# State products on four 64 by 64 quarters of TensorE, with x in two PSUM banks, in a retention, RWKV and Hyena kernel

## The chip, the cores and the metric

One core of one Trainium2 chip. The metric is device time in microseconds of one execution; before the change the median of three runs is 325.34 us (324.66 to 327.6). The profile is that of one further execution.

## What is computed

Three layers follow one another (batch 2, 768 tokens, model width 512 = 8 heads of 64):

```python
# 1: retention with decay, in blocks
intra = (qb @ kb.T * Dmask) @ vb
inter = (qb * lam_pow) @ kv_state
out[block] = intra + inter
kv_state = lam_block * kv_state + (kb * rev_pow).T @ vb
# 2: RWKV channel mix, x_prev is x one token earlier
xk = mu_k * x + (1 - mu_k) * x_prev;  xr = mu_r * x + (1 - mu_r) * x_prev
y = sigmoid(xr @ w_r) * (relu(xk @ w_k) ** 2 @ w_v)
# 3: Hyena: a causal convolution of 5 taps gates a projection
z = (sigmoid(conv(y)) * (y @ w_val)) @ w_out
```

The weights come as float64 and the kernel turns them into float32 itself; products of layers 2 and 3 are made of two float32r parts ("hi" and "lo", three products for one).

## The kernel before

**Tiling.** A chunk is 128 tokens (6 per batch row, 12 in all, numbered 0 to 11), a group is two chunks (256 tokens, 0 to 5). A head pair n (0 to 3) is 128 rows: heads 2n and 2n+1. Chunk 0 of each batch row has no state yet, so chunks 1 to 5 and 7 to 11 have products with a state.

**Attention of a chunk.** Step A (`attention_scores`) transposes k and q (on TensorE for groups 0 to 2, from blocks that a DMA brings, `kin` and `qin`, and a VectorE transpose for the others), decays k (`kt`), makes the scores `sc` and masks them into `p`. Step B (`attention_values`) makes the kv products `u` (L424), the new state (L440) and x (`attend`, L467): first the products of the state with the decayed q (`qd`), 64 rows by 64 columns each, then those of v with p, 128 rows by 64 columns. x of a chunk is one PSUM bank, `x[64*s:64*s+64, n, :]` for head s of pair n; there are two such tiles. `keep_x` (L495) copies it to SBUF.

**Layer 2** for a group: `mix` makes xr and xk from x (xrf, then the parts xrh on ScalarE, L519, and xrl on VectorE or GpSimd, L520), `ffn_r` the products psr, `ffn_k` psk and the squares kk, `ffn_v` psv. All products of layers 2 and 3 stand in `products` (L532), the last in `project` (L671).

**Weights.** w_r and w_k (12 pieces) and w_v (8 pieces) are loaded by `load_w`, one DMA for each piece of 256 rows by 256 columns (L250). A piece is then converted over three ticks: `start` on ScalarE (L167, L168), `bits` on VectorE (L172 to L174), `add` (L179), then whi on ScalarE (L184) and wlo (L187).

**What sets the order.** `LOADS` gives the first DMAs, all in one queue on SyncE. `STEPS` is written by hand: A, B, m, k, M (mixes), r, f, F, h, v (layer 2), t and w (a tick, a load), l (a late weight), G, S, V, P (layer 3); letters behind a number choose the engine. The framework schedules around this list and fixes each engine's order before the run. The loads of chunk c+2, and the 32 block DMAs of a group, are issued inside step A of chunk c (L756, `load_chunk`). Each DMA takes one of eight semaphores in turn, so it also waits until the transfer eight places earlier has landed.

Of the kernel before, what the change touches and what calls it, by code (L numbers as in the profile page):

```python
# [27 lines left out]

LOADS = """
    l k0 v0 q0 k1 q1 w1 M q2 v1 k2 w1 v2 q3 v3 k3 q4 w2 k4 v4 w1 v5 k5 q5 w5  # L30
""".split()
STEPS = """
    W2 c W10 A0vfd tgg A1a tgv B0 B1 A2f x0 B2 tgv A3d tvv tvv B3 m0.0dg tvv m0.1g A4au w m1.0g
    B4 A5af r0.1 r0.0 m1.1g B5 tvg w m2.0 m2.1d k0.0 t r1.0 r1.1 r2.0 t w t w k0.1 r2.1 tv f0.1s
    tvv tgv tvv k1.0 f0.3 k1.1d f0.0s k2.1 w k2.0 w tvv f0.2s tvv F1.1 F1.0sg w tvv w w F1.3s
    tvv F1.2 F2.0s w tvv F2.2s tgv h1.3 tgg F2.3 v0.0 C h1.0 tgv v0.1 F2.1sg A6ad B6v A7ad X
    h1.1 h1.2 v1.0 B7 h2.0 h2.1 x1 v1.1 h2.2 h2.3 v2.0 M3.0g M3.1 v2.1 A8vu A9u f3.3sg f3.1s
    f3.0s f3.2s B8 r3.0 v3.0 r3.1 B9v v3.1 M4.1g M4.0dg l1 r4.1 l1 r4.0 f4.0s A10f f4.1sg l1v
    f4.2s B10v A11au f4.3s G0.0 B11v v4.0 M5.0 M5.1d l1 l1v v4.1 f5.3s Z r5.1 l1 f5.0s r5.0 S0.0
    f5.1sg S1.0v l1 G0.1 f5.2s S0.1v v5.0 G1.0 V0.0 l1v V0.1 G2.1 S1.1v G1.1 P0.1 S3.0v P0.0  # L40
    V1.1 S2.1k V1.0 v5.1 S2.0v G3.1 P1.1 G2.0 S3.1v P1.0v V2.1 G3.0 V2.0 V3.1 G5.1 V3.0 P2.1v
    S5.0 G4.1 P2.0 P3.0 G5.0 S4.1vk S4.0k G4.0 V4.1 V4.0 S5.1vk P3.1 V5.0g V5.1 P4.0v P4.1 P5.0v
    P5.1.2v
# [4 lines left out]
def retention_rwkv_hyena_kernel(  # L48
# [102 lines left out]
    class Conversion:  # L151


        def __init__(self, raw, key=None, hi=None, lo=None, lo_engine=None, add_engine=None):
# [6 lines left out]
            self.add_engine = add_engine or GP  # L161
            self.age = 0
# [7 lines left out]
        def bits(self):  # L170
            x = self.x.bitcast(I32)
            V.tensor_scalar(self.x, self.x, LEAST, MOST, op0=ALU.max, op1=ALU.min)  # L172
# [60 lines left out]
    def load_w(n=1):  # L233
        for _ in range(n):
            if not to_load:
                return
# [8 lines left out]
            else:  # L245
# [4 lines left out]
            last_w[0] = nc.sync.dma_start(  # L250
                raws[key].rearrange("p (k f) -> p k f", k=2),
                sources[name][2 * row * P:(2 * row + 2) * P, 256 * col:256 * col + 256].rearrange(
                    "(k p) f -> p k f", p=P
                ),
            ).ins

    def tick_w(add=GP, lo=GP):
# [7 lines left out]
        else:  # L265
# [5 lines left out]
            lo, add_engine=add,  # L271
# [4 lines left out]
    def tick_late(n=1, lo=GP):  # L276

        for _ in range(n):
# [15 lines left out]
            tick(Conversion(raw, key, whi[key], wlo[key], lo))  # L294
# [4 lines left out]
    def load_qk(g):  # L299
# [3 lines left out]
        group[g] = {}  # L303
        for nm, src in (("k", k), ("q", q)):
            t = group[g][nm + "in"] = att_group_tile(f"{nm}in{g}")
            for n in range(NPAIR):
                for s in range(2):
                    for db in range(2):
                        p0 = 64 * s + 32 * db
                        nc.sync.dma_start(  # L310
                            t[p0:p0 + 32, n, :].rearrange("p (t e) -> p t e", e=32),
                            src[b, 2 * n + s, t0:t0 + G, 32 * db:32 * db + 32].rearrange(
                                "(t r) e -> r t e", r=32
                            ),
                        )
# [6 lines left out]

    def load_kv(c):
        if c % NCH < NCH - 1:
            load_tokens(c, "kt", k, att_tile(f"kt{c}", [P, H, D]))
        load_tokens(c, "vt", v, att_tile(f"vt{c}", [P, H, D]))
# [102 lines left out]
    def state(c):  # L429
# [6 lines left out]
        if cc == 0:  # L436
            V.tensor_copy(new, u)
            return
# [8 lines left out]
    def attend(c, engine):  # L447
# [9 lines left out]
        st = chunk.pop(c)  # L457
        half = [slice(0, 64), slice(64, 128)]
        terms = []
        if cc > 0:  # L460
            terms.append([(half[s], n, state_of[cc % 2][half[s], n, :], st["qd"][half[s], n, :])
                          for n in range(NPAIR) for s in range(2)])
        terms.append([(half[s], n, st["vt"][:, 2 * n + s, :], st["p"][s][:, n, :])
                      for n in range(NPAIR) for s in range(2)])
        for i, term in enumerate(terms):
            for h, n, a, b in term:
                nc.tensor.matmul(  # L467
                    x[h, n, :], a, b, start=(i == 0 and n == 0),
                    stop=(i == len(terms) - 1 and n == NPAIR - 1),
                )  # L470
# [9 lines left out]
    def keep_x(c, x, engine):  # L480
# [9 lines left out]
        for i in range(0, NPAIR, n):  # L490
            dst = xs[g][:, i:i + n, 1 + C * part:1 + C * part + C]
            if engine == "v":
                urgent(V.tensor_copy(dst, x[:, i:i + n]))
            else:
                urgent(nc.scalar.activation(dst, x[:, i:i + n], AF.Copy))  # L495
# [399 lines left out]
```

## Time and profile before

| | |
|---|---|
| Median of the runs | 325.34 us |
| Profiled execution: its own time, its span | 324.76 us, 323.0 us |
| TensorE busy in the span | 300.6 us (93%) |
| VectorE, ScalarE, GpSimd busy | 239.0, 167.9, 87.1 us |
| DMA moved | 29.04 MB |
| Mean granted TensorE clock | 0.968 |

The span is the time from the first to the last instruction, and the execution's own time is a little longer. A matmul of float32 appears as two records. PE is TensorE, DVE VectorE, ACT ScalarE, POOL GpSimd, SP SyncE. Engine shares are means over the whole span; the stretches and timelines below tell more.

### The profile page before, as it was taken

Reading aid. Unit: us, or ns where it says so; the run is one execution under the profiler, and the core shown is the slowest. Engines: PE = TensorE matmul, PEld = TensorE weight load, DVE = VectorE, ACT = ScalarE, POOL = GpSimd, SP = SyncE. Lnnn points to the kernel's source line nnn. Section 1 sums busy time; section 2 is a strip of 40 time slices with the busy share of each in tenths; the row PEclk is TensorE's granted clock in tenths of the full one; section 3 lists DMA queues with packets and bytes.
Section 4 is the critical chain, followed back from the end, with each engine's and each line's share of the span. In section 5 each row is a group of like instructions: output and inputs, shape, how many; then the busy total and the mean of one; then the engine's idle time right before and its main releaser. Section 6 shows DMA issues by size and latency. Waiting matters only on the chain.

```text
span 323.0 us, 6645 instructions
## 1 busy us (share of the span) xinstructions
PE 300.6 (93%) x2660; PEld 281.2 (87%) x2660; DVE 239.0 (74%) x461; ACT 167.9 (52%) x313; POOL 87.1 (27%) x87
## 2 busy tenths in 40 slices
PE   6778779949999999999998999999999999999996
PEld 6666569839999999989998989999999998999985
DVE  5698999689999869887445573499525949999631
ACT  1365894196898343607256244685473345453420
POOL 4254336313000202145127364331620004001010
PEclk9997959958999999999999999999999999999999
DMA  8999973673544302044350120312000010101102
GB/s 154 229 225 276 294 163 59 132 211 92 188 134 80 58 2 65 7 102 87 61 163 19 59 67 2 130 63 68 2 2 1 2 65 0 68 0 67 65 35 98
DMA packets 64957, 29.04 MB, mean 90 GB/s; under 512 B 57090, under 2 KB 57374, under 8 KB 64926
## 3 DMA queue, kind: packets, MB, share of 16 engines
q1 hardware_dynamic: 64926, 28.61, 34.4%
q8 instruction: 21, 0.34, 0.5%
q14 instruction: 10, 0.08, 0.1%
HBM read 25.46 MB, written 3.15 MB: 89 GB/s over the span
## 4 chain that ended last, share of the span: by engine, by line
PE 63%; SPq 14%; DVE 7%; DMA 6%; POOL 4%; issue 3%; ACT 2%; POOLq 0%; DVEq 0%; ACTq 0%
PE psk L532 17%; PE psv L532 16%; PE psa L532 10%; SPq L310 10%; PE pso L671 10%; PE psr L532 5%; SPq L321 3%; DMA kt<-in_k_dram 3%; DMA raw_val<-in_moe_w_val_dram 3%; PE x L467 2%; PE sc L404 1%; DVE wt L174 1%; ACT wt L167 1%; POOL xkl L520 1%; DVE wt L172 1%
## 5 line engine op out<-in xcount | busy, mean ns | idle before, releaser
L532 PE MATMUL psv<-kk,whi_v 128*128 128x256 f32 x384 | 68.2, 279 | 1.0 <-DVE kk L584 1.0
L532 PEld LDWEIGHTS psv<-kk,whi_v 128*128 128x128 f32 x384 | 58.4, 188 | 2.2 <-DVE kk L584 1.4
L532 PE MATMUL psk<-xkl,whi_k 128*128 128x256 f32 x192 | 53.3, 278 | 0.6 <-POOL xkl L520 0.6
L532 PE MATMUL psk<-xkh,whi_k 128*128 128x256 f32 x192 | 53.3, 279 | 0.0
L532 PE MATMUL psk<-xkh,wlo_k 128*128 128x256 f32 x192 | 53.2, 278 | 0.0
L532 PE MATMUL psv<-kk,wlo_v 128*128 128x256 f32 x192 | 53.0, 277 | 0.0
L639 DVE SCALAR_TENSOR_TENSOR gate<-x,cw,gate 128x256 f32<-128x256 f32 x96 | 44.3, 519 | 2.1 <-ACT gate L637 2.1
L532 PEld LDWEIGHTS psk<-xkl,whi_k 128*128 128x128 f32 x192 | 36.1, 188 | 0.9 <-POOL xkl L520 0.8
L532 PEld LDWEIGHTS psk<-xkh,whi_k 128*128 128x128 f32 x192 | 36.0, 188 | 0.4 <-issue 0.2
L532 PEld LDWEIGHTS psk<-xkh,wlo_k 128*128 128x128 f32 x192 | 36.2, 188 | 0.1
L532 PEld LDWEIGHTS psv<-kk,wlo_v 128*128 128x128 f32 x192 | 36.1, 188 | 0.0
L532 PE MATMUL psr<-xrh,whi_r 128*128 128x256 f32 x96 | 27.9, 296 | 1.1 <-ACT xrh L519 1.1
L532 PE MATMUL psr<-xrl,whi_r 128*128 128x256 f32 x96 | 27.7, 289 | 1.3 <-DVE xrl L520 1.3
L532 PE MATMUL psr<-xrh,wlo_r 128*128 128x256 f32 x96 | 27.3, 286 | 0.0
L172 DVE TENSOR_SCALAR wt<-wt 128x512 f32<-128x512 f32 (+1 forms) x29 | 18.4, 641 | 10.8 <-ACT wt L167 10.8
L467 PE MATMUL x<-p,vt 128*64 128x128 f32 x192 | 17.2, 303 | 6.2 <-DVE p L414 6.2
L569 ACT ACTIVATE h<-psk 128x512 f32<-128x512 f32 x24 | 14.3, 595 | 16.3 <-PE psk L532 16.0
L584 DVE TENSOR_TENSOR kk<-h,kk 128x512 fp32r<-128x512 f32 x19 | 14.2, 750 | 10.7 <-ACT h L581 10.7
L467 PEld LDWEIGHTS x<-p,vt 128*64 128x64 f32 x192 | 12.7, 149 | 9.3 <-DVE p L414 7.2
L532 PEld LDWEIGHTS psr<-xrh,whi_r 128*128 128x128 f32 x96 | 18.8, 199 | 2.3 <-ACT xrh L519 1.3
L532 PEld LDWEIGHTS psr<-xrl,whi_r 128*128 128x128 f32 x96 | 18.8, 196 | 1.9 <-DVE xrl L520 1.9
L642 ACT ACTIVATE gate<-gate 128x512 f32<-128x512 f32 x12 | 7.6, 630 | 23.7 <-DVE gate L639 23.7
(138 smaller groups left out, 751.3 us busy)
## 6 DMA issues: line engine op xcount, KB each, us to landing
vt<-in_v_dram SPq DMA_DIRECT2D x12, 256.0 KB, 5.7
kt<-in_k_dram SPq DMA_DIRECT2D x11, 256.0 KB, 4.8
out_dram<-o SPq DMA_DIRECT2D x11, 256.0 KB, 2.0
stage<-in_moe_w_r_dram SPq DMA_DIRECT2D x4, 512.0 KB, 6.2
stage<-in_moe_w_k_dram SPq DMA_DIRECT2D x4, 512.0 KB, 6.4
raw<-in_moe_w_k_dram SPq DMA_DIRECT2D x4, 512.0 KB, 9.1
stage<-in_moe_w_v_dram SPq DMA_DIRECT2D x4, 512.0 KB, 4.3
raw<-in_moe_w_v_dram SPq DMA_DIRECT2D x4, 512.0 KB, 4.1
```

Of the source, the lines that this page charges most:

```text
L167: nc.scalar.activation(self.x, self.full, AF.Abs)
L172: V.tensor_scalar(self.x, self.x, LEAST, MOST, op0=ALU.max, op1=ALU.min)
L174: V.scalar_tensor_tensor(x, self.high, -(1 << 30), x, op0=ALU.bitwise_and, op1=ALU.bitwise_or)
L310: nc.sync.dma_start(t[p0:p0 + 32, n, :].rearrange("p (t e) -> p t e", e=32), src[b, 2 * n + s, t0:t0 + G, 32 * db:32 * db + 32].rearrange( ...
L321: return nc.sync.dma_start(t, src[b, :, t0:t0 + C, :].rearrange("h p d -> p h d"))
L467: nc.tensor.matmul(x[h, n, :], a, b, start=(i == 0 and n == 0), stop=(i == len(terms) - 1 and n == NPAIR - 1),)
L532: nc.tensor.matmul(ps[:, i, :], a, b, start=(first and kk == 0 and n == 0), stop=(last and kk == nk - 1 and n == 2),)
L569: nc.scalar.activation(h, ps, AF.Relu)
L584: (GP if "g" in how else V).tensor_tensor(lo, h, f32(hi), op=ALU.subtract)
L639: V.scalar_tensor_tensor(acc[:, i, :], src, w, acc[:, i, :], op0=ALU.mult, op1=ALU.add)
L642: nc.scalar.activation(acc, acc, AF.Sigmoid)
L671: nc.tensor.matmul(ps, a, w, start=(kk == 0 and i == 0), stop=(kk == KD - 1 and i == 2))
```

## The change

x of a chunk becomes one tile of two PSUM banks, `x[half, n % 2, n // 2, :]`: even pairs in the first bank, odd pairs in the second. For odd pairs the two heads are put on exchanged halves of the partitions. The state products of two pairs (four heads) are written one behind the other, and use the four combinations of row half (where the state and qd lie) and column half (where x goes). There is one x tile in place of two, of the same total size. As x then has exchanged halves in every second 128 rows, the rows of w_r and w_k that multiply them are exchanged on load, and mu_k, mu_r as well: a piece of w_r or w_k takes three DMAs instead of one, mu six instead of two. Step B makes x before u. The loads of later chunks and the blocks become steps of their own (`i`, `j`), and `LOADS` and `STEPS` are written anew. `clamp` lets GpSimd take one operation of a conversion (used once, late); the option "s" of a state is not reached by any step that uses it.

```diff
-        x = ps_s.tile([P, NPAIR, C], F32, name=f"x{c}", tag="x", bufs=2)
+        x = ps_s.tile([P, 2, 4, C], F32, name=f"x{c}", tag="x")
...
-            terms.append([(half[s], n, state_of[cc % 2][half[s], n, :], st["qd"][half[s], n, :])
-                          for n in range(NPAIR) for s in range(2)])
+        for n0 in range(0, NPAIR, 2) if cc > 0 else ():
+            terms += [(half[s ^ n % 2], n, state_of[cc % 2][half[s], n, :],
+                       st["qd"][half[s], n, :]) for n in (n0, n0 + 1) for s in range(2)]
+        terms += [(half[s ^ n % 2], n, st["vt"][:, 2 * n + s, :], st["p"][s][:, n, :])
+                  for n in range(NPAIR) for s in range(2)]
...
+            nc.tensor.matmul(
+                x[o, n % 2, n // 2, :], a, b, start=(o.start, n % 2) not in begun,
+                stop=(o.start, n % 2) not in left,
+            )
...
-            last_w[0] = nc.sync.dma_start(
-                raws[key].rearrange("p (k f) -> p k f", k=2),
+            nc.sync.dma_start(dst[:, 0, :], src[0:P])
+            for i in range(2):
+                last_w[0] = nc.sync.dma_start(
+                    dst[64 * i:64 * i + 64, 1, :], src[P + 64 - 64 * i:P + 128 - 64 * i]
+                ).ins
...
-        kv_products(c)
-        state(c)
-        attend(c, engine)
+        attend(c, "v" if "v" in opt else "")
+        kv_products(c)
+        state(c, opt)
...
-        if c + 2 < B * NCH and f"k{c + 2}" not in LOADS:
-            load_chunk(c + 2)
...
-    W2 c W10 A0vfd tgg A1a tgv B0 B1 A2f x0 B2 tgv A3d tvv tvv B3 m0.0dg tvv m0.1g A4au w m1.0g
+    tgg c W13 W2 tgv A0vfd A1a tgv A2f x0 B0 B1 A3d tvv B2 B3 tvv A4au i6kv j3k m0.0dg tvv m0.1g
```

SyncE's queue behind the first loads, where the last pieces of w_k and the loads for group 3 (chunks 6 and 7) stand. Before (`raw9` and `stage0` are places of w_k pieces, `kin3` and `qin3` the blocks of group 3):

```order
L250 DMA raw9_166<-in_moe_w_k_dram 128x2x256
L321 DMA kt6_521<-in_k_dram 128x8x64
L321 DMA vt6_523<-in_v_dram 128x8x64
L310 DMA kin3_525<-in_k_dram 32x8x32 x16
L310 DMA qin3_542<-in_q_dram 32x8x32 x16
L250 DMA stage0_85<-in_moe_w_k_dram 128x2x256
L321 DMA kt7_631<-in_k_dram 128x8x64
L321 DMA vt7_633<-in_v_dram 128x8x64
L250 DMA stage0_85<-in_moe_w_k_dram 128x2x256
```

With the change:

```order
L260 DMA raw9_188<-in_moe_w_k_dram 64x256 x2
L316 DMA kin3_538<-in_k_dram 32x8x32 x14
L327 DMA kt6_534<-in_k_dram 128x8x64
L327 DMA vt6_536<-in_v_dram 128x8x64
L316 DMA kin3_538<-in_k_dram 32x8x32 x2
L316 DMA qin3_584<-in_q_dram 32x8x32 x16
L258 DMA stage0_85<-in_moe_w_k_dram 128x256
L260 DMA stage0_85<-in_moe_w_k_dram 64x256 x2
L327 DMA kt7_683<-in_k_dram 128x8x64
L327 DMA vt7_685<-in_v_dram 128x8x64
L258 DMA stage0_85<-in_moe_w_k_dram 128x256
L260 DMA stage0_85<-in_moe_w_k_dram 64x256 x2
```

Each piece of w_k is one row of 128 partitions and two of 64 instead of one, and kt and vt of chunk 6 stand behind 14 of the 32 blocks instead of ahead of them all.

VectorE from the decay of chunk 7's kt to the second half of xr of group 2 (`xrl2_1`). Before:

```order
L387 TENSOR_TENSOR kt7_631<-kt7_631,dmask_78 128x512
L172 TENSOR_SCALAR wt_920<-wt_920 128x512
L513 SCALAR_TENSOR_TENSOR xkf0_0_759<-x0_281,rest_177,xkf0_0_759 128x256 x2
L513 SCALAR_TENSOR_TENSOR xkf0_1_882<-x0_281,rest_177,xkf0_1_882 128x256
L173 TENSOR_SCALAR wt_920<-wt_920 128x512
L513 SCALAR_TENSOR_TENSOR xkf0_1_882<-x0_281,rest_177,xkf0_1_882 128x256
L174 SCALAR_TENSOR_TENSOR wt_920<-stage0_85,wt_920 128x512
L520 TENSOR_TENSOR xrl2_0_747<-xrf2_0_741,xrh2_0_746 128x512
L179 ISA stage0_85<-stage0_85,wt_920 128x512x2
L172 TENSOR_SCALAR wt_962<-wt_962 128x512
L440 SCALAR_TENSOR_TENSOR state0_83<-state1_84,pw_79,u7_1702 128x64 x4
L520 TENSOR_TENSOR xrl2_1_756<-xrf2_1_750,xrh2_1_755 128x512
```

With the change:

```order
L388 TENSOR_TENSOR kt7_683<-kt7_683,dmask_78 128x512
L525 SCALAR_TENSOR_TENSOR xkf0_0_941<-x0_342,rest_203,xkf0_0_941 128x256 x2
L525 SCALAR_TENSOR_TENSOR xkf0_1_950<-x0_342,rest_203,xkf0_1_950 128x256 x2
L176 TENSOR_SCALAR wt_933<-wt_933 128x512
L532 TENSOR_TENSOR xrl2_0_804<-xrf2_0_798,xrh2_0_803 128x512
L190 TENSOR_TENSOR wlo_k_2_1_918<-raw9_188,whi_k_2_1_917 128x512
L175 TENSOR_SCALAR wt_962<-wt_962 128x512
L177 SCALAR_TENSOR_TENSOR wt_933<-stage0_85,wt_933 128x512
L532 TENSOR_TENSOR xrl2_1_813<-xrf2_1_807,xrh2_1_812 128x512
L438 COPY state1_84<-u6_1665 128x256
```

The state of chunk 7 and one combination of a conversion (ISA) no longer stand ahead of `xrl2_1`; a subtraction (`wlo_k_2_1`), which GpSimd made before, does.

TensorE where r of group 2 begins. Before:

```order
L404 MATMUL sc0_6_1574<-qT3_1533,kT3_1531 128x128
L404 MATMUL sc1_6_1575<-qT3_1533,kT3_1531 128x128
L424 MATMUL u7_1702<-vt7_633,kt7_631 64x64 x8
L532 MATMUL psr2_0_831<-xrh2_0_746,whi_r_0_0_219 128x256
L532 MATMUL psr2_1_891<-xrh2_0_746,whi_r_1_0_382 128x256
L532 MATMUL psr2_0_831<-xrl2_0_747,whi_r_0_0_219 128x256
```

With the change the kv products of chunk 7 stand here, later, among the products psk of group 0:

```order
L544 MATMUL psk0_1_990<-xkh0_0_946,wlo_k_1_0_759 128x256
L544 MATMUL psk0_1_990<-xkh0_1_955,whi_k_1_1_816 128x256
L425 MATMUL u7_1702<-vt7_685,kt7_683 64x64 x5
L544 MATMUL psk0_1_990<-xkl0_1_956,whi_k_1_1_816 128x256
L544 MATMUL psk0_1_990<-xkh0_1_955,wlo_k_1_1_817 128x256
```

Three more of the eight follow further on. The kv products of chunk 6, which stood between r of group 0 before, now stand around the first two products of r of group 2.

## Rows read from the trace of the kernel before

**Rows 1.** Stretches: length, busy us (instructions) per engine, TensorE clock granted, DMA share, GB/s

```profile
28.00:41.70 13.70, 9.73 (x132) 7.70 (x128) 13.03 (x27) 11.31 (x22) 4.86 (x6) 1.00 1.06 289
...
65.60:75.80 10.20, 6.23 (x36) 5.49 (x37) 9.71 (x19) 9.32 (x19) 2.66 (x2) 0.50 0.54 171
75.80:170.00 94.20, 94.20 (x858) 91.35 (x857) 76.19 (x139) 53.61 (x103) 18.48 (x17) 1.00 0.36 87
170.00:194.00 24.00, 22.43 (x236) 20.80 (x235) 13.73 (x34) 10.82 (x22) 13.57 (x12) 1.00 0.14 45
194.00:319.80 125.80, 125.80 (x985) 119.27 (x983) 84.54 (x158) 60.33 (x110) 24.78 (x18) 1.00 0.11 41
```

**Rows 2.** Timeline of TensorE: start, us, line, operation, [idle before <- releaser]

```profile
67.23 1.12 PE L424 MATMUL u<-vt,kt 128*64 128x64 f32 x16 [3.14 <-DVE wt L172]
69.41 0.79 PE L532 MATMUL psr<-xrh,whi_r 128*128 128x256 f32 x2 [1.07 <-ACT xrh L519]
71.33 0.58 PE L532 MATMUL psr<-xrl,whi_r 128*128 128x256 f32 x1 [1.12 <-DVE xrl L520]
...
74.62 0.58 PE L532 MATMUL psr<-xrl,whi_r 128*128 128x256 f32 x1 [0.15 <-DVE xrl L520]
```

**Rows 3.** Timeline of VectorE, 61 to 75 us

```profile
61.62 1.25 DVE L348 STREAM_TRANSPOSE qT<-qin 128x1024 f32<-128x1024 f32 x1 [2.69 <-DMA qin<-in_q_dram]
...
66.09 0.69 DVE L387 TENSOR_TENSOR kt<-kt,dmask 128x512 f32<-128x512 f32 x1 [1.14 <-DMA kt<-in_k_dram]
...
72.90 1.67 DVE L520 TENSOR_TENSOR xrl<-xrf,xrh 128x512 fp32r<-128x512 f32 x1
```

**Rows 4.** Timelines of ScalarE (three rows) and GpSimd (one), 65 to 75 us

```profile
65.00 0.66 ACT L167 ACTIVATE wt<-stage 128x512 f32<-128x512 f32 x1 [5.63 <-DVE xrf L513]
...
68.74 0.62 ACT L519 ACTIVATE xrh<-xrf 128x512 fp32r<-128x512 f32 x1
...
70.86 0.62 ACT L519 ACTIVATE xrh<-xrf 128x512 fp32r<-128x512 f32 x1
...
72.71 1.31 POOL L187 TENSOR_TENSOR wlo_k<-stage,whi_k 128x512 fp32r<-128x512 f32 x1 [2.92 <-ACT whi_k L184]
```

**Rows 5.** Timeline of SyncE's queue of DMA issues: start, us of issuing

```profile
35.94 4.41 SPq L321 DMA_DIRECT2D vt<-in_v_dram  x1
40.45 10.74 SPq L310 DMA_DIRECT2D kin<-in_k_dram  x16
51.29 8.95 SPq L310 DMA_DIRECT2D qin<-in_q_dram  x16
60.34 0.40 SPq L250 DMA_DIRECT2D stage<-in_moe_w_k_dram  x1
```

**Rows 6.** Timeline of TensorE, a scores stage and chunk 11 in the full stretch

```profile
17.12 0.60 PE L367 MATMUL psqT<-ident,qt 128*128 128x128 f32 x4
...
20.66 1.16 PE L404 MATMUL sc<-qT,kT 64*128 64x128 f32 x16
...
212.29 0.28 PE L532 MATMUL psk<-xkh,wlo_k 128*128 128x256 f32 x1
212.50 1.09 PE L467 MATMUL x<-qd,state 64*64 64x128 f32 x16
213.53 1.09 PE L467 MATMUL x<-p,vt 128*64 128x128 f32 x16
214.55 0.50 PE L532 MATMUL psv<-kk,whi_v 128*128 128x256 f32 x2
```

**Rows 7.** TensorE's waits from 75.8 us on: total, times, longest

```profile
PE psv L532 <- DVE kk L584: 1.0, 2, 0.6
PE psk L532 <- POOL xkl L520: 0.6, 1, 0.6
```

**Rows 8.** Timeline of TensorE, kv products between other products

```profile
133.53 0.56 PE L424 MATMUL u<-vt,kt 128*64 128x64 f32 x10
134.02 0.50 PE L532 MATMUL psv<-kk,whi_v 128*128 128x256 f32 x2
```

More of the change, by code (lines that the diff above doesn't have):

```diff
@@ L427, in kv_products, with state @@
                 )
-    def state(c):
+    def state(c, opt):
         cc = c % NCH
@@ L437, in state @@
             V.tensor_copy(new, u)
+            return
+        if "s" in opt:
+            GP.tensor_tensor(new, old, pw[:, :, C - 1:C].to_broadcast([P, NPAIR, D]), op=ALU.mult)
+            V.tensor_tensor(new, u, new, op=ALU.add)
             return
@@ L455, in attend @@
         assert cc == 0 or c - 1 in kept
-        x = ps_s.tile([P, NPAIR, C], F32, name=f"x{c}", tag="x", bufs=2)
-        st = chunk.pop(c)
+        x = ps_s.tile([P, 2, 4, C], F32, name=f"x{c}", tag="x")
+        st = chunk[c]
         half = [slice(0, 64), slice(64, 128)]
         terms = []
-        if cc > 0:
-            terms.append([(half[s], n, state_of[cc % 2][half[s], n, :], st["qd"][half[s], n, :])
-                          for n in range(NPAIR) for s in range(2)])
[L463 to L470, printed above, removed]
+        for n0 in range(0, NPAIR, 2) if cc > 0 else ():
[3 more added lines that the diff above has]
+                  for n in range(NPAIR) for s in range(2)]
+        begun = set()
+        left = [(o.start, n % 2) for o, n, _, _ in terms]
+        for o, n, a, b in terms:
+            left.pop(0)
+            nc.tensor.matmul(
+                x[o, n % 2, n // 2, :], a, b, start=(o.start, n % 2) not in begun,
+                stop=(o.start, n % 2) not in left,
+            )
+            begun.add((o.start, n % 2))
         keep_x(c, x, engine)
@@ L705, in load @@
             elif nm == "M":
-                nc.sync.dma_start(vec[0:KD], mu_k.rearrange("(n p) -> n p", p=P))
-                then(nc.sync.dma_start(vec[KD:2 * KD], mu_r.rearrange("(n p) -> n p", p=P)))
+                for i, m in enumerate((mu_k, mu_r)):
+                    src = m.rearrange("(a b p) -> b a p", b=2, p=P)
+                    nc.sync.dma_start(vec[KD * i:KD * i + KD:2], src[0])
+                    for j in range(2):
+                        then(nc.sync.dma_start(
+                            vec[KD * i + 1:KD * i + KD:2, 64 * j:64 * j + 64],
+                            src[1, :, 64 - 64 * j:128 - 64 * j],
+                        ))
             elif nm == "w":
@@ L763, in attention_scores, with attention_values @@
         mask(c)
-    def attention_values(c, engine):
+    def attention_values(c, opt):
+        attend(c, "v" if "v" in opt else "")
         kv_products(c)
-        state(c)
-        attend(c, engine)
-    def load_chunk(c):
-        g, part = divmod(c, CPG)
-        if g < PE_GROUPS:
-            for nm in "kqv":
-                load_part(nm, c)
-        else:
-            with tc.issue_after(last_w[0]):
-                load_kv(c)
-                if part == 0:
-                    load_qk(g)
+        state(c, opt)
     def convolution_weights():
@@ L813, in step @@
                         stack.enter_context(tc.issue_after(ins))
-                tick_w(*num, *engines)
+                tick_w(*num, *engines, clamp=GP if "c" in opt else V)
+        elif nm == "i":
+            with tc.issue_after(last_w[0]):
+                for o in opt:
+                    load_part(o, *num)
+        elif nm == "j":
+            with tc.issue_after(last_w[0]):
+                load_blocks(*num, opt)
         elif nm == "W":
```

88 lines of the change are left out of this document (44 added, 44 removed).

## Prediction

> **What bounds the kernel now.** I read the stages first, then the waits of the engine that each stage shows as full, then the queue behind those waits. The table of stretches [rows 1] splits the span. From 75.80 us to 319.80 us TensorE is busy for all but 1.57 us (24.00 - 22.43, between 170 and 194 us), and the waits of that stretch have three entries only [rows 7]: two for the subtraction that ends a kk tile, one for an xkl on GpSimd. Behind it lie 3.2 us for the last copy and store. So the last 244 us are a list of products: only fewer or shorter products, or an earlier start, shorten them. [...]
>
> What does the start of the full stretch wait for? TensorE's rows [rows 2]: from the kv products of chunk 7 on it waits 3.14 us, 1.07 us, 1.12 us and 0.15 us, and runs on from 74.62. The last three gate r of group 2 and name xrh on ScalarE and xrl on VectorE; the second xrl ends at 74.57 (72.90 + 1.67) [rows 3]. On VectorE this second xrl stands behind the decay of kt of chunk 7, which waited for its transfer until 66.09, and behind the state of chunk 7; it took 1.67 us where the decay, an operation of the same size, took 0.69, and it lay beside a GpSimd subtraction from 72.71 for 1.31 us [rows 4]. ScalarE stood 5.63 us until 65.00 [rows 4]. The row names xrf for that, but this instruction does not read xrf: it reads the w_k piece whose transfer SyncE issued at 60.34 [rows 5], so I take the piece's landing as the releaser. That piece, and kt of chunk 7 right behind it, stand in SyncE's queue behind 32 block transfers for group 3, issued from 40.45 to 60.24 (51.29 + 8.95) [rows 5].
>
> So three places count: the full stretch, VectorE's rows around 66 to 75 us, and SyncE's rows ahead of them.
>
> **State products.** One chunk's products with the state are 8 matmuls, 16 records. In the full stretch they take 1.03 us (212.50 to 213.53), those with p 1.02 us (213.53 to 214.55) [rows 6]. Four records of a full array take 0.60 us, a single one 0.28, so one starts about every 0.11 us. Sixteen in a row would need 15 x 0.11 + 0.28 = 1.93 us, but they take 1.09 us in their row: two already run at a time. That holds where the two lie on row halves with two banks (scores, 16 in 1.16 us), on column halves (p), and on the diagonal with one bank (state). The change uses all four quarters; nothing in the trace shows four at once. Bounds: nothing, if quarters take turns, and 8 steps of 0.11 becoming 4, 0.44 us per chunk. I take 0.44, because the two ways of pairing that it combines (scores, p) both show full overlap. Ten chunks have such products. Chunks 1 to 5 run ahead of 75 us, where TensorE waits for VectorE: worth nothing. Chunks 7 to 11 lie in the full stretch: 5 x 0.44 = **-2.2 us**.
>
> [...] In this trace the state's two row halves write one bank and still run two at a time (1.09 us against 1.93). [...]
>
> **One x tile instead of two.** A chunk's first product now waits until the x before it is copied out. In the full stretch 27 or more products of 0.11 us lie between any two x tiles in the new order, 3 us: free. In the early stage chunk 1 waits for a copy on ScalarE, hidden behind VectorE's queue; if not, it meets the slack of 3.8 us below.
>
> **Order at the start of the full stretch.** VectorE's new rows have the second xrl without the state ahead of it, and the GpSimd subtraction that lay beside it is VectorE's own now, behind it. With the w_k piece at 65.00 as now, ScalarE's new rows have the first xrh one conversion earlier in the list (before it ended at 68.74 + 0.62 = 69.36) and the second behind the same work (70.86 + 0.62 = 71.48) [rows 4]. The second xrl (0.69, as the decay) follows: 71.5 to 72.2, I take 71.9 instead of 74.57, 2.7 us earlier. But TensorE is then at 0.50 clock, and the rows show the level rise at 75.80, 4.5 us after the products of r began again at 71.33. In the new order they begin at about 69.5, so I let the clock rise near 74.0: as much is done by then as by 75.80 before, a gain of **-1.8 us**. Ends: -1.3 if the clock stays down until 75.8 (3.9 us of products at half speed instead of 1.2), -2.9 if it rises by 72.4.
>
> **Moved into the full stretch.** The kv products of chunk 7, at 67.23 before, now stand among psk and psv. The array changes shape 42 times instead of 36 behind that point; a change costs 0.10 us (212.29 to 212.50 is 0.21, where a step of such products is 0.11) [rows 6]: **+0.6**. Ten records of kv products took 0.49 us in the full stretch (133.53 to 134.02) [rows 8], one change among it, so 16 cost 1.6 x 0.39: **+0.6**. The wait for POOL's xkl (0.6 us) should go, since xk and xr of the half used first now come first on GpSimd: **-0.6** (end: 0). The two kk waits (1.0) I leave.
>
> **Transfers.** Every w_r or w_k piece is three issues instead of one, mu six instead of two: 26 more ahead of the kt of chunk 7. The blocks' rows give 0.5 us per issue (8.95 us for 16), 13 us if nothing hid them. Up to 45 us the transfers themselves are full (the DMA share from 28.00 to 41.70 is 1.06 [rows 1]), so I cost the extra issues there at nothing: the data behind them takes longer. Each transfer waits for the one eight places earlier, so small ones leave less in flight; around the six of mu I expect about 1 us of empty queue, which VectorE's waits absorb. Behind 42 us, kt and vt of chunk 6 move behind 14 blocks, and the w_k piece has three issues: four more issues, 2.0 us. Against that, vt of chunk 6, whose issue held the queue for 4.41 us from 35.94 [rows 5], no longer stands ahead of the blocks; but these then follow twelve transfers of w_k of which only eight may be on the way, so I expect them to begin about when they do now. I take the piece's landing as unchanged, +-1.5 us. VectorE reaches the decay of chunk 7 with about 4 us to spare before (2.69 + 1.14 us of waiting [rows 3]); the order's rows ahead of that place hold the same work but for one more conversion step, so that slack covers both.
>
> The three extra warm-up products are six records of 0.11 us, 0.7 us ahead of the first transposes; q now lands before v, which brings the next transposes forward, and the slack of 3.8 us covers the rest. Nothing.
>
> **Sum.** Against the profiled execution's 324.76 us (span 323.0 and 1.76 around it, 0.58 under the median of 325.34): -2.2 - 1.8 + 0.6 + 0.6 - 0.6 = -3.4, so **321.4 us**.
>
> **Rivals.**
> *Quarters take turns.* The state's products stay at 1.03 us: 321.4 + 2.2 = 323.6 us. For it: no row shows four at a time, and the two heads of a pair share a bank. Against it: today's pairs share one as well and overlap. [...]
> *The full stretch starts no earlier.* If the w_k piece lands 2.5 us later, or the clock stays down, the 1.8 us go: 323.2 us. For it: the piece is now three transfers behind 34.
> *Slower: SyncE's issues become the bound.* The place is the w_k piece that releases ScalarE at 65.00. Half of the 13 us of added issues unhidden lands it 6.5 us later; the second xrl follows at 78.4 instead of 71.9, 3.8 us later than the 74.57 of before: 324.76 + 3.8 - 1.6 (the other terms) = 327.0 us; with all of the 13 us 333.5 us. It decides once the piece is more than 4.3 us late (landing at 69.3). Against it: up to 41.70 the queue is full of data, not of issues.
> *Better.* Clock back by 72.4 (-1.1), kk waits gone too (-1.0), changes of shape hidden (-0.6): 318.7 us.
>
> **Chances.** Forecast 0.42 (its own range 319.8 to 323), turns 0.17, no earlier start 0.14, slower 0.14, better 0.13. One per cent of 325.34 is 3.3 us, about what a measurement of this kernel tells from no change: faster is below 322.1, slower above 328.6. Faster: 0.13, of the forecast 0.31, and 0.07 from the two middle rivals: 0.51. Slower: that part of its rival where the piece is over 8.1 us late, 0.08. The rest, 0.41, lies within 1%. The range leaves out half of the better and half of the slower case: 318.5 to 327.0.
>
> **What would show it.** Right: the state's 8 products in the full stretch from 1.03 us to about 0.6; the second xrl ends near 72 us; no GpSimd subtraction beside it; the ScalarE row that waits for the w_k piece starts within 1.5 us of 65.00. Wrong: that row at 69 us or later; the state's products still in 1.0 us; new TensorE waits behind 80 us for an x copy, a kk or a w_v piece, which an earlier start would bring out where VectorE has little room.

## The result, and the profile after

Eighteen runs of each kernel: 328.28 us median (326.78 to 329.57) with the change, 325.69 us before (323.27 to 327.89). The ratio is 1.0083, 95% interval 1.0056 to 1.0110: slower by 0.8%, where 321.4 us was forecast and 327.0 was the range's end. The profiled execution took 326.96 us (span 325.2), 2.2 us more than that of before.

The stretches of the changed kernel (start:end, length, busy us and instructions of TensorE, its weight loads, VectorE, ScalarE, GpSimd, granted clock, DMA share (the mean busy share of the core's 16 DMA engines), GB/s), for [rows 1]:

```profile
8.00:12.00 4.00, 2.36 (x36) 1.94 (x36) 2.62 (x10) 0.60 (x1) 1.06 (x1) 1.00 0.43 117
28.00:41.70 13.70, 9.70 (x122) 7.84 (x124) 13.67 (x26) 9.45 (x20) 6.38 (x6) 0.88 1.13 235
65.60:79.70 14.10, 8.71 (x68) 7.91 (x67) 12.54 (x26) 9.23 (x19) 0.00 (x0) 0.76 0.77 189
79.70:322.10 242.40, 241.35 (x2089) 230.21 (x2088) 177.51 (x340) 122.91 (x227) 64.81 (x46) 1.00 0.22 60
```

The last line holds the answer: the full stretch is shorter than before (242.4 us to the last product, 244.0 before), but it begins at 79.7 instead of 75.8. At both places the same products are done, but for one of 115 records psr from xrh and the kv products of chunk 7, which now lie behind that point. So +3.9 us at the start and -1.6 us behind it make the +2.3 us.

TensorE at the start of the full stretch and at chunk 11, for [rows 2, 6]:

```profile
74.12 0.80 PE L544 MATMUL psr<-xrh,whi_r 128*128 128x256 f32 x2 [4.98 <-ACT xrh L531]
74.84 0.91 PE L425 MATMUL u<-vt,kt 128*64 128x64 f32 x12
75.68 0.58 PE L544 MATMUL psr<-xrl,whi_r 128*128 128x256 f32 x1
...
215.27 0.67 PE L475 MATMUL x<-qd,state 64*64 64x128 f32 x16
215.86 1.09 PE L475 MATMUL x<-p,vt 128*64 128x128 f32 x16
```

The state set now takes 0.59 us (215.27 to 215.86) instead of 1.03, while the p set keeps its 1.09. But r of group 2 begins at 74.12 instead of 69.41. What it waits for is xrh on ScalarE, and ScalarE stood behind the w_k piece, for [rows 4]:

```profile
70.25 0.66 ACT L170 ACTIVATE wt<-stage 128x512 f32<-128x512 f32 x1 [5.78 <-DMA stage<-in_moe_w_k_dram]
...
73.44 0.62 ACT L531 ACTIVATE xrh<-xrf 128x512 fp32r<-128x512 f32 x1
...
75.99 0.62 ACT L531 ACTIVATE xrh<-xrf 128x512 fp32r<-128x512 f32 x1
```

The piece landed 5.25 us later than before (70.25 against 65.00). SyncE's queue shows how it came to that, for [rows 5]:

```profile
42.55 1.29 SPq L260 DMA_DIRECT2D raw<-in_moe_w_k_dram  x2
43.97 8.97 SPq L316 DMA_DIRECT2D kin<-in_k_dram  x14
52.99 0.45 SPq L327 DMA_DIRECT2D kt<-in_k_dram  x1
53.48 0.58 SPq L327 DMA_DIRECT2D vt<-in_v_dram  x1
54.12 1.56 SPq L316 DMA_DIRECT2D kin<-in_k_dram  x2
55.79 9.23 SPq L316 DMA_DIRECT2D qin<-in_q_dram  x16
65.12 0.39 SPq L258 DMA_DIRECT2D stage<-in_moe_w_k_dram  x1
65.56 1.12 SPq L260 DMA_DIRECT2D stage<-in_moe_w_k_dram  x2
```

The blocks begin at 43.97 instead of 40.45; with kt and vt among them and three issues for the piece, its last part goes out near 66.7 instead of 60.7. In the full stretch one wait is left, for [rows 7] (engine, line, releaser: us in total, times, longest):

```profile
PE psk L544 <- DVE x L615: 1.0, 1, 1.0
```

### The profile page after: what moved, and what is told of

It reads as the page before. It is cut to its first block, busy times and chain, and to the rows that moved or that the text cites. A ratio compares the mean times of both kernels' runs of the same rounds, so it can differ in the third digit from the quotient of the medians.

```text
span 325.2 us, 6731 instructions
## 1 busy us (share of the span) xinstructions
PE 297.7 (92%) x2666; PEld 279.0 (86%) x2666; DVE 242.5 (75%) x468; ACT 165.6 (51%) x308; POOL 90.8 (28%) x85
## 3 DMA queue, kind: packets, MB, share of 16 engines
HBM read 25.46 MB, written 3.15 MB: 88 GB/s over the span
## 4 chain that ended last, share of the span: by engine, by line
PE 75%; SPq 14%; DMA 6%; ACT 2%; issue 2%; POOL 1%; DVE 0%; ACTq 0%
PE psk L544 21%; PE psv L544 20%; PE psa L544 10%; PE pso L683 10%; PE psr L544 8%; SPq L327 4%; SPq L316 4%; DMA raw<-in_moe_w_k_dram 4%; PE x L475 3%; SPq L260 2%; PE sc L405 2%; SPq L258 2%; DMA stage<-in_moe_w_k_dram 1%; PE u L425 1%; DMA lam_t<-in_lam_dram 1%
## 5 line engine op out<-in xcount | busy, mean ns | idle before, releaser
L651 DVE SCALAR_TENSOR_TENSOR gate<-x,cw,gate 128x256 f32<-128x256 f32 x96 | 42.4, 502 | 4.1 <-ACT gate L649 4.1
L596 DVE TENSOR_TENSOR kk<-h,kk 128x512 fp32r<-128x512 f32 x20 | 16.1, 803 | 6.9 <-ACT h L593 6.7
L175 DVE TENSOR_SCALAR wt<-wt 128x512 f32<-128x512 f32 (+1 forms) x28 | 13.3, 474 | 8.5 <-ACT wt L170 8.4
L683 PE MATMUL pso<-whi_out,gh 128*128 128x512 f32 (+1 forms) x52 | 19.5, 375 | 0.0
L683 PE MATMUL pso<-wlo_out,gh 128*128 128x512 f32 (+1 forms) x52 | 19.5, 374 | 0.0
L544 PEld LDWEIGHTS psr<-xrh,wlo_r 128*128 128x128 f32 x96 | 19.4, 202 | 0.0
```

Source lines behind the costliest of these rows:

```text
L175: self.clamp.tensor_scalar(self.x, self.x, LEAST, MOST, op0=ALU.max, op1=ALU.min)
L544: nc.tensor.matmul(ps[:, i, :], a, b, start=(first and kk == 0 and n == 0), stop=(last and kk == nk - 1 and n == 2),)
L596: (GP if "g" in how else V).tensor_tensor(lo, h, f32(hi), op=ALU.subtract)
L651: V.scalar_tensor_tensor(acc[:, i, :], src, w, acc[:, i, :], op0=ALU.mult, op1=ALU.add)
L683: nc.tensor.matmul(ps, a, w, start=(kk == 0 and i == 0), stop=(kk == KD - 1 and i == 2))
```

## The experiments

All times are given as ratios to the kernel before on the same chip, in the same comparison. "Piece" is the start of the ScalarE row that waits for the w_k piece, "clock up" the time at which the granted clock rises to 1.00 for good; both are from the one profiled execution of each kernel. The changed kernel's ratio is that of the result above.

| kernel | ratio (95%) | piece | clock up |
|---|---|---|---|
| before | 1 | 65.00 | 75.8 |
| changed | 1.0083 (1.0056 to 1.0110) | 70.25 | 79.7 |
| w_whole | 0.9957 (0.9932 to 0.9982) | 65.84 | 75.2 |
| three_full | 1.0016 (0.9981 to 1.0051) | 67.64 | 76.9 |
| dummy_issues | 1.0085 (1.0050 to 1.0119) | 70.13 | 77.3 |
| regroup | 1.0149 (1.0090 to 1.0208) | 71.63 | 81.6 |
| by_k | 0.9932 (0.9894 to 0.9970) | 65.45 | 75.2 |
| diagonal | 1.0171 (1.0131 to 1.0211) | 70.32 | 79.6 |
| before_split | 1.0462 (1.0404 to 1.0520) | 73.62 | 89.1 |
| before_quarters | 1.0285 (1.0232 to 1.0338) | 62.94 | 82.0 |
| before_one_x | 1.0336 (1.0254 to 1.0417) | 63.54 | 82.7 |
| mu_whole | 1.0213 (1.0150 to 1.0277) | 67.02 | 83.3 |
| swap_heads | 0.9984 (0.9952 to 1.0017) | 65.10 | 77.6 |
| swap_heads_mu6 | 1.0110 (1.0045 to 1.0175) | 66.30 | 78.7 |
| copy_back | 1.0165 (1.0087 to 1.0244) | 64.23 | 79.4 |
| late_quarters | 0.9992 (0.9955 to 1.0029) | 65.06 | 74.2 |
| late_quarters_new | 0.9926 (0.9892 to 0.9960) | 65.45 | 74.0 |

### Is the gain that of the quarters?

**diagonal.** The changed kernel without the exchange:

```diff
-            terms += [(half[s ^ n % 2], n, state_of[cc % 2][half[s], n, :],
+            terms += [(half[s], n, state_of[cc % 2][half[s], n, :],
...
```

> The changed kernel with both heads of every pair on their own halves again (no exchange; x still in two banks, the DMAs as many and as small as in the changed kernel), so the products with a state use only the two quarters on the diagonal. If four quarters run at a time in the changed kernel because of the exchange, a set of these products takes 1.0 to 1.1 us again instead of 0.6, and the time is 2.2 to 2.6 us above the changed kernel. If the shorter sets come from the two banks alone, or from the order of the products, nothing changes.

A state set of diagonal in the full stretch:

```profile
194.72 1.09 PE L475 MATMUL x<-qd,state 64*64 64x128 f32 x16
```

Back to 1.09 us, with two banks and the order of the products kept; the full stretch starts at the same time (79.6), and the ratio rises by 0.9% (1.0171 against 1.0083), about 2.8 us, with an interval of about 1.6. In the profiled executions the last product ends 2.3 us later (324.4 against 322.1). So it is the four quarters that shorten the sets, and they are worth what the prediction gave them.

### Is the loss that of the split transfers?

**w_whole.** One transfer for each piece, 24 fewer; no other engine's order changes:

```diff
...
-            nc.sync.dma_start(dst[:, 0, :], src[0:P])
-            for i in range(2):
-                last_w[0] = nc.sync.dma_start(
-                    dst[64 * i:64 * i + 64, 1, :], src[P + 64 - 64 * i:P + 128 - 64 * i]
-                ).ins
+            last_w[0] = nc.sync.dma_start(dst, src.rearrange("(k p) f -> p k f", p=P)).ins
```

> The changed kernel with each piece of w_r and w_k loaded by one DMA again, so 20 fewer... counted exactly 24 fewer issues ahead of chunk 8; the rows of w_r and w_k are then not exchanged, so its output is another. mu keeps its six DMAs. The order of the instructions on TensorE, VectorE, ScalarE and GpSimd stays exactly that of the changed kernel. Theory A: the w_k piece that released ScalarE at 70.25 lands 3 to 4 us earlier, and the time is 324 to 325.5 us against 328.3 (the six issues of mu, about 1.5 us, remain). Theory B: 327.5 to 328.5, as the changed kernel.

**before_split.** The kernel before with the same split, mu's six transfers with it, rows not exchanged:

```diff
...
+            nc.sync.dma_start(dst[:, 0, :], src[0:P])
+            for i in range(2):
+                last_w[0] = nc.sync.dma_start(
+                    dst[64 * i:64 * i + 64, 1, :], src[P + 64 * i:P + 64 * i + 64]
+                ).ins
...
```

> The kernel before, with each piece of w_r and w_k loaded by three DMAs instead of one and mu by six instead of two (26 more issues, no exchange, all else as before). Theory A (the added issues on SyncE made the changed kernel start its full stretch late): the last piece of w_k lands about 5 us later than the 65.0 of before, the full stretch starts 4 to 5 us later, and the time is 329 to 331 us against 325.7. Theory B (the new order of loads and steps is what starts late): within 1 us of before.

w_whole is 1.26% faster than the changed kernel by the two ratios, about 4.1 us; the piece is back at 65.84. So the split transfers are the loss of the changed kernel, and theory B (the new lists as such) falls. before_split loses 4.6%, about three times the most that was expected, but this is not the price of the split alone. The framework sorted the work anew: ScalarE's copy of chunk 5's x and its part of xrf, at 57.92 and 58.46 us before, stand at 74.75 and 75.75, behind the conversion that waits for the piece until 73.62.

### Number of issues, or half of the partitions?

Theory A said: the number. **regroup** asks for it. x takes heads 0 to 3 on its lower half and 4 to 7 on its upper; a piece then needs two transfers, mu two:

```diff
...
+            for o in range(2):
+                last_w[0] = nc.sync.dma_start(
+                    dst[64 * o:64 * o + 64],
+                    src[o, :, 2 * row:2 * row + 2, 256 * col:256 * col + 256],
+                ).ins
...
```

> The changed kernel with other heads on exchanged places: x takes heads 0 to 3 on its lower half and 4 to 7 on its upper half (heads of one row half still go to different banks, four quarters as before), so that a piece of w_r or w_k needs two transfers instead of three and mu two instead of six: 16 issues fewer, same bytes. The order of work on all other engines stays. Theory A (number of issues): half of the 4.1 us that one transfer for each piece gave back, and about 1.6 us for mu, so 324.5 to 325 us where the kernel before takes 325.7 (ratio 0.996 to 0.998). Theory T (64-partition transfers are slow in themselves, the number does not matter): at most 1 us below the changed kernel (ratio 1.005 to 1.008).

With 16 issues fewer the ratio rose to 1.0149, outside of what either theory had said. Its interval still overlaps that of the changed kernel, but piece and clock are later too, by 1.4 and 1.9 us. Its stretches:

```profile
8.00:12.00 4.00, 2.73 (x39) 2.21 (x39) 3.74 (x10) 0.56 (x2) 0.51 (x1) 1.00 1.07 223
38.00:42.00 4.00, 4.00 (x49) 3.33 (x42) 3.97 (x7) 2.98 (x7) 1.39 (x1) 0.50 1.05 235
```

From 8 to 12 us the queue is full again (1.07 against 0.43 in the changed kernel, whose six issues of mu stand there). But from 38 to 42 us, where only w_k moves, a full queue (1.05) brings 235 GB/s. The same stretch of w_whole brings 365 GB/s with no more (0.99):

```profile
38.00:42.00 4.00, 2.42 (x42) 2.03 (x44) 3.95 (x8) 3.99 (x10) 0.63 (x3) 0.88 0.99 365
```

In regroup each transfer of w_r and w_k goes to 64 partitions. **by_k** changes that alone, against regroup: as many issues, the same bytes, the same order on every engine row by row, but 128 partitions:

```diff
...
-            for o in range(2):
-                last_w[0] = nc.sync.dma_start(
-                    dst[64 * o:64 * o + 64],
-                    src[o, :, 2 * row:2 * row + 2, 256 * col:256 * col + 256],
-                ).ins
+            for k in range(2):
+                last_w[0] = nc.sync.dma_start(dst[:, k, :], src[P * k:P * k + P]).ins
```

> The kernel of the regrouped heads again (two transfers for each piece of w_r and w_k, two for mu), but each of the two transfers goes to all 128 partitions with 256 columns, where it went to 64 partitions with 2 x 256 (the rows are then not the ones that x needs, so its output is another). Same number of issues, same bytes, and the order on every engine is the same row by row. Theory H (a transfer to half of the partitions moves at a lower rate: all of w at 228 GB/s and 0.149 us for a packet of 2 KB in the regrouped kernel, 401 GB/s and 0.085 us with whole pieces): packets of 2 KB take 0.09 to 0.10 us around 40 us, the full stretch starts 4 to 6 us earlier than at 81.6, and the ratio to before is 0.998 to 1.004 instead of 1.015. Theory A alone (only the number of issues counts): as the regrouped kernel, 1.011 to 1.018.

```profile
38.00:42.00 4.00, 3.32 (x56) 2.72 (x56) 3.97 (x8) 3.24 (x7) 1.46 (x2) 1.00 1.02 345
```

345 GB/s, the piece 6.2 us earlier (65.45 against 71.63), the clock up 6.4 us earlier, and a ratio of 0.9932 against 1.0149; the intervals lie far apart. By the trace's records of packets, one of 2 KB took 0.087 us on average from 40 to 42 us in by_k and 0.148 in regroup. Theory H is shown: the transfers to half of the partitions moved at about two thirds of the rate (235 of 345 GB/s).

SyncE issued regroup's transfers to the two halves in turn (eight in 5.15 us from 36.18), and with both halves asked for it moved those 235 GB/s, against 345 in by_k, 365 in w_whole and 374 in the kernel before, all from 38 to 42 us. The two kernels of the result differ in the same sense: from 40 to 42 us a packet of 2 KB took 0.086 us on average before and 0.124 in the changed kernel, where two of the three transfers of a piece go to 64 partitions.

**three_full** has the number of the changed kernel without the halves:

```diff
-                    dst[64 * i:64 * i + 64, 1, :], src[P + 64 - 64 * i:P + 128 - 64 * i]
+                    dst[:, 1, P * i:P * i + P], src[P:2 * P, P * i:P * i + P]
```

> The changed kernel with as many transfers as it has (three for each piece of w_r and w_k, six for mu), but each of the three goes to all 128 partitions: 256 columns of the first 128 rows, then twice 128 columns of the other 128 rows (the rows are not exchanged, so its output is another; a third of w moves in packets of 1 KB instead of 2). The order on every other engine is that of the changed kernel row by row. Theory H (half of the partitions, half of the rate): most of the 1.26% between the changed kernel and the one with whole pieces comes back, ratio 0.996 to 1.001. Theory A (the number of issues): 1.006 to 1.010, as the changed kernel.

```profile
38.00:42.00 4.00, 2.63 (x55) 2.03 (x50) 3.95 (x8) 3.99 (x10) 0.68 (x3) 1.00 0.92 269
```

A little outside of the range given for theory H. The piece is 2.6 us earlier than in the changed kernel and 1.8 us later than in w_whole. So of the 4.4 us between those two the halves are 2.6, and 1.8 go to the number of issues. The packets of 1 KB are no reason: one took 0.046 us from 40 to 42 us, one of 2 KB 0.088. How the issues cost the 1.8 us is not shown; SyncE's issues of w_k take about 0.45 us each here, and the share from 38 to 42 us is 0.92 where w_whole has 0.99. The clock comes up at 76.9, between 75.2 and 79.7, and the ratios divide the 1.26% in about the same way (0.67 and 0.59, each with an interval of some 0.4).

**dummy_issues.** Whole pieces, and two tiny transfers behind each:

```diff
...
+            for i in range(2):
+                j = 2 * (len(raws) - 1) + i
+                last_w[0] = nc.sync.dma_start(
+                    dummy[64 * i:64 * i + 64, j:j + 1], src[64 * i:64 * i + 64, 0:1]
+                ).ins
```

> The changed kernel with one transfer for each piece of w_r and w_k, and behind each two further transfers of 64 single values into a tile that nobody reads: as many issues as in the changed kernel, but the pieces whole (rows not exchanged, so its output is another). Theory A (the issues themselves): as slow as the changed kernel, ratio to before 1.006 to 1.012. Theory T (small pieces move slowly): as fast as with whole pieces, ratio 0.994 to 0.998.

The number expected of theory A came (1.0085), but it settles less than it seems to: the framework sorted the work anew (in the trace over 100 of VectorE's 468 operations stand in other places), and of eight transfers on their way most are now tiny. SyncE's row of the last four tiny issues takes 3.15 us from 42.85, and the blocks begin at 46.14, later than in the changed kernel (43.97). Since three_full has as many issues and the piece 2.5 us earlier, the number alone is not what holds the piece until 70.13 here.

**mu_whole.** Only mu by two transfers:

```diff
...
-                    for j in range(2):
-                        then(nc.sync.dma_start(
...
+                nc.sync.dma_start(vec[0:KD], mu_k.rearrange("(n p) -> n p", p=P))
```

> The changed kernel with mu loaded by two transfers as before instead of six (its odd rows are then not exchanged, so its output is another); w_r and w_k stay split. Theory A: the empty queue at 8 to 12 us (53 and 181 GB/s there against 274 and 254 before) goes, and the time falls by 1.5 to 2 us, ratio to before 1.002 to 1.004. Rival: the lag is taken up by waits of VectorE further on, less than 0.5 us, ratio 1.007 to 1.009.

A miss, and not by the transfers: the piece came 3.2 us earlier (67.02), as theory A wants, but r of group 2 started at 78.24. The framework had sorted the work anew: the copy of chunk 5's x and xrf stand behind the first steps of the piece's conversion (xrf ends at 74.96 on VectorE), and xrh, at 77.56 on ScalarE, behind three more steps of w_k and a sigmoid. What mu costs by itself is read from the pair below.

### Why is the old list worse with the quarters?

**before_quarters.** The kernel before, its lists and whole transfers, with the attend and keep_x of the changed kernel:

```diff
-        x = ps_s.tile([P, NPAIR, C], F32, name=f"x{c}", tag="x", bufs=2)
+        x = ps_s.tile([P, 2, 4, C], F32, name=f"x{c}", tag="x")
...
```

> The kernel before, with its own lists of loads and steps and one DMA for each piece of w_r and w_k and for mu, but x in two banks with exchanged heads and the state products on four quarters (the rows of w_r and w_k are not exchanged, so its output is another). Theory A: only the gain is left, 5 sets of 0.49 us in the full stretch: 323 to 323.7 us against 325.7, and the start of the full stretch stays where it was, within 1 us. Rival: one x tile instead of two, or the new order that the framework makes of it, costs as much: 325 to 326 us.

**before_one_x.** The kernel before with one x tile of one bank:

```diff
-        x = ps_s.tile([P, NPAIR, C], F32, name=f"x{c}", tag="x", bufs=2)
+        x = ps_s.tile([P, NPAIR, C], F32, name=f"x{c}", tag="x")
```

> The kernel before with one x tile of one bank instead of two such tiles, nothing else. It asks why the four quarters on the old lists were 10 us slower. If the cause is the single tile (a chunk's first product waits for the copy of the x before it, and the framework sorts the work around it anew): 8 to 10 us slower than before, ratio 1.024 to 1.031, with a wait of TensorE for an x copy on ScalarE near 49 us. If it is something in the quarters (two banks, exchanged order of the products): within 1 us of before.

before_quarters took 2.9% more, where its theory A wanted 0.6 to 0.8% less. before_one_x, without any quarter, loses 3.4%, a little above its range, and both show the same wait of 3.0 us for an x copy. The longest waits of before_one_x behind 40 us:

```profile
PE psr L532 <- ACT xrh L519: 4.7, 1, 4.7
PE x L467 <- DVE p L414: 3.2, 2, 2.2
PE x L467 <- ACT x L495: 3.0, 1, 3.0
```

TensorE waits 3.0 us for the copy of chunk 4's x, which stands on ScalarE behind a conversion. The wait itself is not the whole loss (7 us at the start): the framework sorts VectorE's and ScalarE's work anew, and xrf of group 2 ends at 71.99 us on VectorE instead of 64.95, although the piece is earlier (63.54). The prediction had the one tile as free.

### Can the gain be had?

**swap_heads** exchanges the heads in k and q, so that w needs no exchange; **swap_heads_mu6** has four more issues of mu, with the same order on all engines; **copy_back** undoes the exchange where x is copied out. A part of each change, in this order:

```diff
+    def head(n, s):
+        return 2 * n + (s ^ n % 2)
...
+                for s in range(2):
+                    nc.tensor.matmul(
+                        ps[64 * s:64 * s + 64, n, :], src[:, head(n, s), :], ident, ...
```

```diff
+                    src = m.rearrange("(a b p) -> b a p", b=2, p=P)
+                    nc.sync.dma_start(vec[KD * i:KD * i + KD:2], src[0])
```

```diff
+            for a, b, j in ((slice(0, P), slice(0, P), 0), (lo, up, 1), (up, lo, 1)):
...
+                    urgent(nc.scalar.activation(dst[a, j], src[b, j], AF.Copy))
```

> The changed kernel, its lists kept, with the exchange moved from x to k and q: for odd pairs k and q are brought with exchanged heads (two products with the unit matrix instead of one transpose for groups 0 to 2, other blocks for groups 3 to 5), so the state and qd are exchanged and x comes out in its natural order. w_r, w_k and mu need no exchange: one transfer for each piece, as before the change. If the late start is all that the change lost: the gain of the quarters is left, ratio 0.990 to 0.996. Rival: the framework, which sorts the work anew for other products and transfers, makes an order that starts late all the same: 1.00 to 1.02.

> As the kernel that exchanges k and q, but mu still by six transfers (natural rows): the order on the engines is the same row by row, only four issues more ahead of the first pieces of w_r. It asks what the issues of mu cost by themselves: 1.5 to 2 us if the empty queue at 8 to 12 us is passed on to the start of the full stretch, nothing if waits of VectorE take it up.

> The changed kernel with the exchange undone where x is copied out of PSUM: three copies for one (the odd pairs' halves apart), w_r, w_k and mu whole and natural. If the transfers are the loss, ratio 0.992 to 0.998, less what the added copies (about 0.3 us each on ScalarE, 2 for each chunk and 4 for a second chunk of a group) put on ScalarE ahead of 75 us. Rival: the new order or the copies start it late: 1.00 to 1.02.

swap_heads (0.9984, between its two ranges) has the piece where before has it (65.10), but starts r of group 2 at 72.61: its rival, the framework's new order, takes what the transfers gave back. Four issues of mu cost 1.2 us at the piece and 1.1 us at the clock (78.7 against 77.6), of the 1.5 to 2 us expected; the median moves by more (1.3%), which the one profiled execution of each does not explain. copy_back loses by its order and the added copies (TensorE waits up to 5.1 us for an x copy ahead of 60 us).

**late_quarters** and **late_quarters_new** leave the start alone. Quarters only for chunks 6 to 11, whose k and q come as blocks, in which the exchange is another source row; chunks 0 to 5 keep two x tiles. The second has the new lists:

```diff
+    def head(c, n, s):
+        return 2 * n + (s ^ (n % 2 if c >= NCH else 0))
...
-                            src[b, 2 * n + s, t0:t0 + G, 32 * db:32 * db + 32].rearrange(
+                            src[b, head(CPG * g, n, s), t0:t0 + G, 32 * db:32 * db + 32].rearrange(
...
+        elif c == NCH:
+            x_stack.close()
+            x_pool[0] = ctx.enter_context(tc.tile_pool(name="ps_x2", bufs=1, space=PSUM))
```

> The kernel before with its own lists and transfers, and with the four quarters in batch row 1 alone (chunks 6 to 11, the only ones whose products lie in the full stretch): there the heads of odd pairs are exchanged in k and q by the block transfers that bring them anyway, so x comes out in its natural order, in one tile of two banks; chunks 0 to 5 keep two tiles of one bank and the diagonal. The order of TensorE is that of the kernel before for its first 242 rows. If the loss of the changed kernel lies ahead of the full stretch alone: 5 sets of 0.49 us are left, ratio 0.990 to 0.994. Rival: the one tile of two banks, or the order that the framework makes of it, costs as much in the full stretch: 0.998 to 1.003.

> The same quarters in batch row 1 alone, whole transfers and two x tiles for chunks 0 to 5, with the lists of loads and steps of the changed kernel. If the new lists are worth something by themselves (no wait for an xkl or a kk in the full stretch), it is up to 1 us faster than the one with the old lists, ratio 0.987 to 0.992. Rival: the framework sorts the start anew and it starts late: 0.995 to 1.01.

On the old lists nothing is gained (0.9992). The state sets of the full stretch give 2.1 us, but TensorE's waits there grow, for [rows 7] (late_quarters):

```profile
PE psv L565 <- DVE kk L617: 1.8, 2, 1.5
...
PE psk L565 <- POOL xkl L553: 1.3, 1, 1.3
```

These were 1.0 and 0.6: TensorE is earlier at the same two places, VectorE and GpSimd are not, so 1.5 us go there. The profiled span is 0.5 us shorter than before, about what is left; what took back the 1.6 us by which the clock rose earlier (74.2) is not traced. On the new lists those waits are but one of 0.8 us (kk; the first two rows below lie ahead of 74.0), the clock comes up at 74.0, and the kernel takes 321.8 us where before takes 324.03 in that comparison: 0.9926, with nothing of the computation left out, and faster than both kernels. That is 2.1 us better than late_quarters, where up to 1 us was expected of the new lists.

```profile
PE psr L564 <- ACT xrh L551: 1.8, 1, 1.8
PE psk L564 <- ACT xkh L551: 1.4, 1, 1.4
PE psv L564 <- DVE kk L616: 0.8, 1, 0.8
```

## Why the prediction was wrong, step by step

**What bounds the kernel:** right. A list of products from 75.8 us on, and a start that hangs on VectorE, ScalarE and the w_k piece. The whole difference is found in these two places.

**State products:** right. -2.2 us forecast; the five sets took 5.46 us in all and take 2.99, so -2.5. The rival in which quarters take turns fell with it. The two heads of a pair still share a bank in the changed kernel, each with its own half of the partitions, and its eight products took 0.59 us all the same (a row of 0.67 us, where diagonal with the same two banks has one of 1.09).

**Behind the start:** the sum was right, its parts less so. Forecast -2.2 + 0.6 + 0.6 - 0.6 = -1.6, measured 243.95 to 242.39 us, -1.56. The kv products cost 0.9 instead of 0.6, the changes of shape show at the scores (+0.75). Both kk waits went, which had been left in (-1.0), and a new one of 1.0 came for a VectorE product that frees a PSUM tile. That these errors cancel is luck.

**One x tile:** with the new lists, whose steps make x ahead of u, nothing speaks against the price of nothing in the full stretch: TensorE waits for an x copy only once in the changed kernel, 1.8 us until 40.26. But no run varies the tiles alone there. With the old lists one tile costs 7 us at the start (before_one_x), by a mechanism that the prediction had named (the copy on ScalarE) and thought covered by slack.

**Order at the start:** right in form. The second xrl ends 7.1 us behind the piece (77.34 - 70.25; forecast 6.9), with no GpSimd subtraction beside it. The clock rose 5.6 us behind the first product of r; 4.5 were forecast. The term of -1.8 does not fit its own ends: worked out as they are, a rise at 74.0 gives about -2.2. With the piece late this decided nothing.

**Transfers:** the step that failed. "I take the piece's landing as unchanged, +-1.5 us"; it came 5.25 us late, and the term of -1.8 became +3.9. Of the 5.25 us, 2.6 go to the transfers to half of the partitions (three_full against the changed kernel), 1.8 to the number of issues (w_whole against three_full), and 0.8 are there with whole pieces too (65.84 against 65.00) and were not taken apart. The step gave a transfer to 64 partitions no other rate than one to 128, and two of its sentences were wrong.

The added issues up to 45 us were costed at nothing because the DMA share was 1.06; but that share says that the engines are busy, not what they move. In the changed kernel it was 1.13 from 28 to 41.7 us at 235 GB/s, where before has 289 at 1.06 and w_whole 262 at 0.94. three_full, with as many issues but whole width, has 234 GB/s there too, at a share of 0.94: the added issues leave the queue less than full, so "nothing" was wrong for them as well.

And the blocks were expected "about when they do now", since eight transfers may be on their way; they began 3.5 us later. That is mostly the number of issues: three_full begins them at 43.15, w_whole at 37.01. The halves show behind their first 14: kt of chunk 6 is issued at 52.99 in the changed kernel, at 50.62 in three_full and at 48.95 in w_whole, and the piece keeps these distances.

**Rivals:** what came is the one on the other side, given 0.14: its place, and its point of decision (a landing behind 69.3), were right, and its 327.0 us stands against 326.96 profiled and 328.28 median. That it comes so near is luck: it was worked out for a piece 6.5 us late and a second xrl at 78.4, and the piece came 5.25 us late, the second xrl at 77.34. Its cause was put down to unhidden issues alone; by the runs that is the smaller part (1.8 of 4.4 us). The rates by which the halves could have been priced were in the trace of before only as whole transfers (374 GB/s from 38 to 42 us) and as blocks to 32 partitions, which were bound by their issues (57 to 81 GB/s from 44 to 60 us, at a share of 0.35 to 0.47); no row there had a transfer to 64 partitions, and the range should have had a bound for it. Why the median lies 1.3 us above the profiled execution stays open; that of before lies 0.9 us above its own.

## What to carry to other kernels

In this kernel a transfer to half of the partitions was not half a transfer (235 GB/s in regroup against 345 in by_k, with as many issues and bytes). Try a split by columns or rows in which each part still goes to all 128, as in by_k, or move the exchange to where data is brought in small blocks anyway, as in late_quarters_new (0.9926). A full DMA share did not tell the rate here (a share of 1.05 moved 235 GB/s in regroup, one of 0.99 moved 365 in w_whole); price a changed transfer by GB/s at that share, and follow the queue to the piece that releases the next engine. Gains in the full stretch and losses at the start are best read apart, at a point where both kernels have done the same products.

## What was not expected of the hardware

The rate of half-partition transfers: 235 GB/s (regroup, 38 to 42 us) at a DMA share of 1.05, against 345 to 374 to 128 partitions (by_k, w_whole and the kernel before), and 0.148 us (regroup) against 0.087 (by_k) for a packet of 2 KB from 40 to 42 us. The order that the framework fixes is worth as much as any of this: with transfers that land earlier (mu_whole, before_one_x) the full stretch started 3.6 to 6.9 us later.
